# What the first tile's logits wait for, and the order of these logits, the rest columns and the third V tile in a fused attention/MLP kernel

## Chip, cores, metric

One core of one Trainium2 chip. The metric is device time of one execution in microseconds (us); lower is better. "TensorE" is PE in the profile, its weight loads are PEld, VectorE is DVE, ScalarE is ACT.

## The reference, cut to what matters

```python
q, k, v = split(x @ wqkv)                      # x: 2048 x 512, 32 heads of 16
pq = einsum("bhsd,hdf->bhsf", q, w_phi)        # logits of q
pk = einsum("bhsd,hdf->bhsf", k, w_phi)        # logits of k
phi = concat(softmax(p), softmax(-p))          # for both
kv, z = phi_k^T v, sum_s phi_k                 # linear attention
o  = (phi_q kv) / (phi_q z + 1e-6) @ wo
b  = relu(x @ w1) @ w2
return g * o + (1 - g) * b                     # g = sigmoid(x . gate_w)
```

`x @ wq @ w_phi` is computed as `x @ (wq w_phi)`: the kernel first folds `w_phi` into the q and k weights. (Each softmax has 15 free logits after subtracting the last one, so a folded matrix is 512 x 480.)

## The kernel before: the parts that matter

All engines' instructions are written in a fixed order; semaphores order them across engines. Blocks of 128 token rows are "tiles" (16 of them). The kernel's matmuls write into banks of a memory called PSUM (`PS`); an *evacuation* is the copy of such a result to a tile in the main on-chip memory (SBUF), from which the later matmuls read. A *folding* is one piece of the product `wq w_phi` or `wk w_phi`. Four pieces of TensorE work meet at the end of the start-up:

- `pre(i)`, eight foldings: `i` 0 to 3 give the q weights, 4 to 7 the k weights. Each has four matmuls of 120 columns into one PSUM bank (0, 1, 6, 7 in turn) and one evacuation to `WQK`, on DVE for even `i` and on ScalarE for odd `i`.
- `vtile(m)`: the V rows of tile `m`, four matmuls of 512 columns, one copy.
- `rest(0)`: the last 96 columns of the first MLP layer with the gate column for tokens 0 to 511, sixteen matmuls of 97 columns.
- `atile(0)`: the q and k logits of tile 0, eight matmuls of 480 columns, into PSUM bank 0 (q) and bank 1 (k).

```python
def pre(i):
    which, dt = i // 4, i % 4
    bank = (0, 1, 6, 7)[i % 4]
    dst = WQK[:, which, dt * DE:(dt + 1) * DE]
    ...                                   # four matmuls into PS[:, bank, 0:DE], event pm{i}
    if i % 2 == 0:
        p.op("dve", lambda e: e.tensor_copy(dst, PS[:, bank, 0:DE]), after=[f"pm{i}"], ev=f"pc{i}")
    else:
        p.op("act", lambda e: e.activation(dst, PS[:, bank, 0:DE], ACT.Copy),
             after=[f"pm{i}"], ev=f"pc{i}")
    free[bank] = [f"pc{i}"]               # who uses the bank next waits for this

def atile(m):
    first = xready(m // 4) + ([f"pc{i}" for i in range(8)] if m == 0 else [])
    order = [(dt, w) for dt in range(NDT) for w in range(2)]     # q, k, q, k, ...
    ...
    for i, (dt, which) in enumerate(order):
        p.op("pe", ...matmul(PS[:, which, 0:DE], XT[:, dt, tile], WQK[:, which, dt]),
             after=(first if i == 0 else []) + (free[which] if dt == 0 else []), ...)
    ...                                   # exponentials on ScalarE after all eight

# the order of the program there
hunit(0, 8); hunit(0, 9, "dve")
vtile(0, "dve"); vtile(1, "act", nextbank())
for i in range(4): pre(i)
rest(0)
for i in range(4, 8): pre(i)
vtile(2, "dve")
for m in range(NT): atile(m) ...
```

So the first logit matmul waits for all eight evacuations, because q and k alternate.

The softmax here doesn't subtract the row's maximum and nothing guards it: scores larger than these inputs give would overflow.

## Time and profile before

| | before |
|---|---|
| median of the first three runs | 147.69 us (147.18 to 147.95) |
| span of the profiled run | 146.8 us |
| PE busy | 143.2 us, 98% |
| share of PE in the chain that ended last | 95% |

From the page of the kernel before: the span, busy time by engine, and the chain that ended last by engine.

```profile
span 146.8 us, 2520 instructions
...
PE 143.2 (98%) x961; PEld 73.2 (50%) x978; DVE 92.3 (63%) x157; ACT 72.7 (49%) x125; POOL 52.0 (35%) x62
...
PE 95%; DMA 2%; DVE 1%; issue 1%; SPq 0%
```

TensorE is the limit from end to end. In such a kernel a change of order can win only what TensorE loses by waiting, so the question is where it waits. The view of waits of the kernel before has one line for the place of the change (who waited for whom: us in total, times, longest):

```profile
PEld PS L336 <- DVE WQK L321: 0.4, 1, 0.4
```

L336 is the logit matmuls, L321 the DVE evacuations of the folded weights. It is the weight *load* that waits 0.4 us, and loads normally run ahead of their matmuls, so most of it hides. The view names DVE, but see below: ScalarE's last evacuation ended later. The timeline of the kernel before shows the surroundings (start, duration, engine, line, operation, count, and in brackets the idle time before it):

```profile
16.23 1.00 PE L316 MATMUL PS<-Wbd,PHQ 128*128 128x120 bf16 x16
...
17.07 0.86 PE L294 MATMUL PS<-W,XT 128*128 128x97 bf16 x16
...
17.77 1.00 PE L316 MATMUL PS<-Wbd,PHQ 128*128 128x120 bf16 x16
...
18.18 1.22 DVE L321 CAST WQK<-PS 128x480 bf16<-128x480 f32 x2 [0.31 <-PE PS L316]
18.41 1.04 ACT L323 ACTIVATE WQK<-PS 128x480 bf16<-128x480 f32 x2
...
18.82 0.81 PE L411 MATMUL PS<-WV,XT 128*128 128x512 bf16 x3
19.56 1.34 PEld L336 LDWEIGHTS PS<-WQK,XT 128*128 128x128 bf16 x8 [0.42 <-DVE WQK L321]
19.59 1.78 PE L336 MATMUL PS<-WQK,XT 128*128 128x480 bf16 x8
```

Read down it: q folding, rest columns, k folding, V tile (one of its four records is missing), logits. The k evacuations end at 18.18 + 1.22 = 19.40 (DVE) and 18.41 + 1.04 = 19.45 (ScalarE), and the logits' load starts just behind, at 19.56. ScalarE came last: in the instruction records a semaphore instruction that waits for ScalarE stands in front of the load, and the load itself waits for DVE. The matmul line has no bracket, because a matmul's recorded duration (0.38 us for 512 columns) is longer than the time after which the next can start (0.216 us), so a short pause is covered by a modelled end. The chain of waits has the same blindness; of the kernel before it shows no pause there:

```profile
17.93 0.84 PE PS L316 x16
18.77 0.05 issue
18.82 0.81 PE PS L411 x3
19.63 1.74 PE PS L336 x8
```

The pause is seen only when the starts are compared: the last V matmul starts at 19.252, the first logit at 19.592, 0.340 us later, where 0.216 is the pitch, the usual time from one start to the next. That is 0.124 us lost.

### The profile page before, as it was taken

The numbers are of one execution on the slowest core, as the hardware profiler recorded it, in microseconds if no ns is written. First come the engines' busy times: TensorE is split into PE (matmuls) and PEld (weight loads), VectorE is DVE, ScalarE is ACT, GpSimd is POOL, SyncE is SP. The second block draws the span as 40 slices with busy tenths as digits, with TensorE's granted clock in tenths as the row PEclk, the third lists the DMA queues.
The fourth block names the chain that finished last, engine by engine and source line by source line (L and its number), as shares of the span: only waits on it lengthen the run. The fifth ranks groups of instructions, "written<-read, shape, count | busy, mean of one in ns | idle before, by whom it ended". The sixth has DMA issues, their size and how long they took to land.

```text
span 146.8 us, 2520 instructions
## 1 busy us (share of the span) xinstructions
PE 143.2 (98%) x961; PEld 73.2 (50%) x978; DVE 92.3 (63%) x157; ACT 72.7 (49%) x125; POOL 52.0 (35%) x62
## 2 busy tenths in 40 slices
PE   8999999999999999999999999999999999999994
PEld 3444744444545545555645555554444444444443
DVE  3327746777688778678698976675444555555342
ACT  3307547887778778877878863022222111111150
POOL 2040001788768678787868820300000000000000
DMA  6999991033449965335843531454343322322213
GB/s 197 295 258 214 180 263 23 0 71 71 76 86 304 178 198 92 71 71 107 43 107 71 107 71 21 90 107 110 74 94 82 75 71 67 80 71 74 71 44 106
DMA packets 45221, 16.12 MB, mean 110 GB/s; under 512 B 39352, under 2 KB 44568, under 8 KB 45208
## 3 DMA queue, kind: packets, MB, share of 16 engines
q1 hardware_dynamic: 45056, 15.92, 49.6%
q8 instruction: 8, 0.13, 0.4%
q10 hardware_dynamic: 152, 0.03, 0.1%
q14 instruction: 5, 0.04, 0.1%
HBM read 4.41 MB, written 2.10 MB: 44 GB/s over the span
## 4 chain that ended last, share of the span: by engine, by line
PE 95%; DMA 2%; DVE 1%; issue 1%; SPq 0%
PE PS L490 25%; PE PS L282 19%; PE PS L336 18%; PE PS L499 9%; PE PS L411 9%; PE PS L528 5%; PE PS L465 3%; PE PS L433 3%; DMA OT<-in_A_x_dram 2%; PE PS L294 2%; PE PS L316 1%; PE PS L239 1%; DVE WQK L513 1%; DVE XT L255 0%; SPq L162 0%
## 5 line engine op out<-in xcount | busy, mean ns | idle before, releaser
L490 PE MATMUL PS<-W,HT 128*128 128x512 bf16 (+4 forms) x181 | 40.0, 366 | 0.3
L379 POOL TENSOR_TENSOR EB<-EB,SC 128x1024 bf16<-128x1024 bf16 x15 | 28.9, 1927 | 25.0 <-DVE SC L377 25.0
L355 ACT ACTIVATE EB<-PS 128x480 bf16<-128x480 f32 (+1 forms) x44 | 30.1, 757 | 15.1 <-PE PS L336 15.1
L504 ACT ACTIVATE TFA<-PS,GT 128x512 bf16<-128x512 f32 x16 | 11.0, 687 | 42.7 <-PE PS L499 36.6
L282 PE MATMUL PS<-XT,W 128*128 128x512 bf16 x124 | 30.0, 379 | 0.2
L336 PE MATMUL PS<-WQK,XT 128*128 128x480 bf16 x128 | 28.5, 366 | 0.0
L375 DVE TENSOR_REDUCE ZB<-EB 128x64 f32<-128x1024 bf16 x15 | 18.3, 1220 | 14.0 <-ACT EB L355 14.0
L513 DVE SCALAR_TENSOR_TENSOR WQK<-PS,OMG,TFA 128x512 bf16<-128x512 f32 (+2 forms) x17 | 12.2, 719 | 23.6 <-ACT TFA L504 22.4
L490 PEld LDWEIGHTS PS<-W,HT 128*128 128x128 bf16 (+1 forms) x187 | 17.0, 98 | 17.4
L268 ACT ACTIVATE HT<-PS 128x512 bf16<-128x512 f32 x35 | 20.3, 616 | 7.6 <-PE PS L528 5.7
L336 PEld LDWEIGHTS PS<-WQK,XT 128*128 128x128 bf16 x128 | 12.5, 98 | 14.0 <-DVE WQK L321 0.4
L390 DVE TENSOR_REDUCE ZB<-EB 128x64 f32<-128x1024 bf16 x16 | 18.6, 1164 | 0.0
L282 PEld LDWEIGHTS PS<-XT,W 128*128 128x128 bf16 x128 | 12.0, 98 | 13.2
L399 POOL TENSOR_TENSOR EB<-EB,SC 128x512 bf16<-128x512 bf16 x16 | 16.9, 1056 | 1.3
L499 PE MATMUL PS<-WO,OT 128*128 128x512 bf16 x63 | 16.0, 378 | 0.1
L411 PE MATMUL PS<-WV,XT 128*128 128x512 bf16 x59 | 15.3, 378 | 0.3
L475 DVE TENSOR_TENSOR WQK<-PS,RDEN 128x512 bf16<-128x512 f32 x16 | 11.1, 691 | 0.5
L499 PEld LDWEIGHTS PS<-WO,OT 128*128 128x128 bf16 x64 | 6.1, 97 | 7.2
L421 ACT ACTIVATE VS<-PS 128x512 bf16<-128x512 f32 x14 | 8.5, 610 | 2.0 <-PE PS L411 2.0
L377 DVE RECIPROCAL SC<-ZB 128x64 f32<-128x64 f32 x16 | 8.9, 553 | 0.5
L528 PE MATMUL PS<-XT,W 128*128 128x512 bf16 x31 | 7.9, 400 | 0.1
L411 PEld LDWEIGHTS PS<-WV,XT 128*128 128x128 bf16 x64 | 5.5, 97 | 4.9
(57 smaller groups left out, 87.2 us busy)
## 6 DMA issues: line engine op xcount, KB each, us to landing
out_dram<-WQK SPq DMA_DIRECT2D x15, 128.0 KB, 1.7
W<-in_B_w_dram SPq DMA_DIRECT2D x3, 256.0 KB, 4.5
W<-in_B_w_dram SPq DMA_DIRECT2D x2, 384.0 KB, 5.3
OT<-in_A_x_dram SPq DMA_DIRECT2D x2, 256.0 KB, 3.0
WV<-in_A_wqkv_dram SPq DMA_DIRECT2D x1, 512.0 KB, 6.3
W<-in_B_w_dram SPq DMA_DIRECT2D x1, 512.0 KB, 4.5
WO<-in_A_wo_dram SPq DMA_DIRECT2D x2, 256.0 KB, 3.0
W<-in_B_w_dram SPq DMA_DIRECT2D x1, 352.0 KB, 5.8
```

The lines of the kernel that those rows point to most:

```text
L268: p.op("act", lambda e: e.activation(dst, src, ACT.Relu), after=[f"h{c}_{kt}"], ev=ev)
L282: p.op("pe", lambda e, t=t: e.matmul(PS[:, bank, :], W1[:, t, kt * P:(kt + 1) * P], XT[:, t, c * 512:(c + 1) * 512], start=(t == 0), stop= ...
L336: p.op("pe", lambda e, dt=dt, which=which: e.matmul(PS[:, which, 0:DE], XT[:, dt, m * P:(m + 1) * P], WQK[:, which, dt * DE:(dt + 1) * DE] ...
L355: p.op("act", lambda e: e.activation(dst, s_, ACT.Exp, scale=scale), after=[f"qk{m}"] + busy, ev=ev)
L375: p.op("dve", lambda e: e.tensor_reduce(zk, ek, AX.X, ALU.add), after=[emk, f"cst{b}"], ev=f"zk{m}")
L379: p.op("pool" if m < NT - 1 else "dve", lambda e: e.tensor_tensor(EB[:, b, 3, :].rearrange("p (g f) -> p g f", f=DH), EB[:, b, 2, :].rearr ...
L390: p.op("dve", lambda e: e.tensor_reduce(ZB[:, b, 0:64].rearrange("p (h s) -> p h s", s=2), bass.AP(tensor=EB, offset=base, ap=[[EBS, P], [ ...
L399: p.op("pool", lambda e: e.tensor_tensor(EB[:, b, 0, :].rearrange("p (h s f) -> p h s f", h=H, s=2)[:, :, 1, :], EB[:, b, 1, :].rearrange( ...
L411: p.op("pe", lambda e, dt=dt: e.matmul(PS[:, bank, :], XT[:, dt, m * P:(m + 1) * P], WV[:, dt, :], start=(dt == 0), stop=(dt == NDT - 1)), ...
L490: p.op("pe", lambda e, kt=kt, M=M: e.matmul(PS[:, bank, 0:n], HT[0:M, kt, m * P:(m + 1) * P], W2[0:M, kt, cs], start=(kt == 0), stop=(kt = ...
L499: p.op("pe", lambda e, t=t: e.matmul(PS[:, bank, :], OT[:, t, m * P:(m + 1) * P], WO[:, t, :], start=(t == 0), stop=(t == NDT - 1)), after ...
L528: p.op("pe", lambda e, u=u: e.matmul(PS[:, UB[u], :], W1[:, t, u * P:(u + 1) * P], XT[:, t, 0:512], start=(t == 0), stop=(t == NDT - 1)), ...
```

## The change

Its intent: let the first logits wait only for what they use. In tile 0 the four q matmuls come ahead of the four k matmuls, and each group waits for its own four evacuations. The q logits are written to bank 0, so through `free[0]` they also wait for that bank's last user, the first k folding `pre(4)`, to be evacuated. The third V tile moves between the two foldings, and the rest columns behind the k folding.

```diff
@@ atile
-            first = xready(m // 4) + ([f"pc{i}" for i in range(8)] if m == 0 else [])
+            first = xready(m // 4)
             order = [(dt, w) for dt in range(NDT) for w in range(2)]
             if m - 1 in split:
                 order = [(dt, w) for w in (1, 0) for dt in range(NDT)]
+            if m == 0:
+                order = [(dt, w) for w in (0, 1) for dt in range(NDT)]
             for i, (dt, which) in enumerate(order):
                 ...
-                    after=(first if i == 0 else []) + (free[which] if dt == 0 else []),
+                    after=(first if i == 0 else []) + (free[which] if dt == 0 else [])
+                    + ([f"pc{4 * which + c}" for c in range(4)] if m == 0 and dt == 0 else []),
@@ order of the program
         for i in range(4):
             pre(i)
-        rest(0)
+        vtile(2, "dve")
         for i in range(4, 8):
             pre(i)
-        vtile(2, "dve")
+        rest(0)
```

## The prediction

> **What bounds the kernel.** TensorE issue. The page gives PE busy 143.2 of 146.8 us (98%); the chain that ended last is 95% PE, and its pieces follow one another from 3.97 us on without a wait for another engine. In the instruction records a 512-column matmul starts 216 ns after the one before, a 480-column one 202 ns, a folding one (120 columns) 52 ns, a rest one (97 columns) 43 ns. (The Trainium skill, TensorE: Matmul & The Clock Gate, Back-to-back issue gap, gives N/2.4 + 2.5 ns when warm, 215.8 ns at 512; this trace agrees.)
>
> Comparing all start-to-start times with these pitches leaves one real gap after 12 us. (Others, 217 ns each with weight loads running on, are missing records.) It is where the change acts: the third V tile's last matmul starts at 19.25, so the first logit matmul is due at 19.47, but starts at 19.59: 0.12 us lost. It waits for the last two evacuations of folded k weights: DVE ends 19.40, ScalarE 19.45, then a semaphore instruction at 19.49, the load at 19.56, the matmul at 19.59. The view of waits has this as PEld waiting 0.4 us for DVE WQK L321, most of which is only a load that could not run ahead.
>
> **What the change does.** It removes and adds no work. From 16.23 (folding) the same matmuls run in another order: 16 x 52 + 4 x 216 + 16 x 52 + 16 x 43 ns = 3.24 us, so the first logit is due at 19.47 again. Worked out from the trace's durations:
> - V tile 17.07 to 17.93; its DVE copy starts 0.42 us after its last matmul starts (as before): 18.14 to 18.83.
> - k folding 17.93 to 18.77. DVE evacuates at 18.75-19.40 and 19.33-19.98 (behind the V copy, 0.6 us later than before); ScalarE at 18.58-19.15 and 19.03-19.62.
> - rest columns 18.77 to 19.47, taken by ScalarE from 19.66, where it was idle until 21.41.
> - q logits at 19.47: q weights are done by 17.95, but PSUM bank 0 was used by the first k folding, evacuated by DVE about 19.40. So the load still waits, just, for one semaphore: 19.47 to 19.52.
> - k logits due 0.81 us later, 20.28; their weights are done by 19.98.
>
> **On the critical path.** 0.07 to 0.12 us of TensorE time, nothing else. The first exponential moves from 21.41 to about 21.30. Everything behind is issue-bound with slack elsewhere: the next x chunk, read at 22.07, landed at 18.9, the k weights for the folding at 15.3. So the 0.1 us should survive to the end.
>
> **Predicted time.** 147.69 - 0.1 = 147.6 us, range 147.0 to 148.1 (three runs of before spread over 0.77 us, far more than the gain). Faster by over 2%: 1%; within 2%: 98%; slower by over 2%: 1%.
>
> **What would show it.** Right: in the timeline the first logit matmul near 19.5, the q ones followed without a pause by the k ones at 20.3; the wait of PEld for DVE WQK shrunk; span near 146.7. Wrong: a pause between q and k logits (k evacuation later than 20.2); a pause before the q logits as long as before; or the first exponential at 21.4.
>
> **What would make it wrong.** Bank 0 freed later than I work out, because the V copy delays the DVE queue: then the gain shrinks to nothing or a loss of 0.1 us. Input DMAs jittering more than here, where the old order had slack elsewhere. Later phases answering the 0.1 us shift with a new wait. None of these comes near 2%.

## The result, and the profile after

The change ran at 147.12 us median (146.99 to 147.26, six runs), before at 147.33 us (147.17 to 147.95, six runs). The ratio of the two is 0.9978, with a 95% interval of 0.9957 to 0.9999: "same" at 2%, barely below 1. Ratios here are the mean time of one kernel's fast runs over that of the other's of the same rounds, so not quite the ratio of the medians.

From the page of the changed kernel:

```profile
span 145.7 us, 2520 instructions
...
PE 142.1 (98%) x961; PEld 72.7 (50%) x978; DVE 92.2 (63%) x157; ACT 72.8 (50%) x125; POOL 52.0 (36%) x62
...
PE 97%; DVE 1%; issue 1%; ACT 0%; DVEq 0%
```

Its timeline at the same place (lines there are numbered 2 to 3 higher than before from the logits on: L338 is the logits, L414 the V tiles):

```profile
15.27 1.00 PE L316 MATMUL PS<-Wbd,PHQ 128*128 128x120 bf16 x16
...
16.11 1.03 PE L414 MATMUL PS<-WV,XT 128*128 128x512 bf16 x4
...
16.97 1.00 PE L316 MATMUL PS<-Wbd,PHQ 128*128 128x120 bf16 x16
17.17 0.69 DVE L422 CAST VS<-PS 128x512 bf16<-128x512 f32 x1 [0.27 <-PE PS L414]
17.59 1.03 ACT L323 ACTIVATE WQK<-PS 128x480 bf16<-128x480 f32 x2 [0.60 <-PE PS L316]
...
17.78 1.21 DVE L321 CAST WQK<-PS 128x480 bf16<-128x480 f32 x2
17.81 0.86 PE L294 MATMUL PS<-W,XT 128*128 128x97 bf16 x16
18.48 1.34 PEld L338 LDWEIGHTS PS<-WQK,XT 128*128 128x128 bf16 x8
18.51 1.78 PE L338 MATMUL PS<-WQK,XT 128*128 128x480 bf16 x8
```

The wait of PEld for L321 is gone from the view of waits; the load has no bracket. The last rest matmul starts at 18.462 and takes 0.043 us, so the first logit was due at 18.505; it started at 18.506. The DVE evacuation line, however, ends at 17.78 + 1.21 = 18.99, half a microsecond *after* the q logits began: it holds two evacuations, of which the q logits need only the first (bank 0, ended at 18.428). The chain of waits now runs rest columns into logits:

```profile
17.14 0.84 PE PS L316 x16
17.98 0.69 PE PS L294 x16
18.67 1.62 PE PS L338 x8
```

The whole span differs by 1.1 us, though. A table by stage, with starts of matmuls from the instruction records, says where:

| stage | before, us | change, us | difference |
|---|---|---|---|
| start of program to first folding matmul | 16.231 | 15.269 | -0.962 |
| first folding matmul to first q logit | 3.361 | 3.237 | -0.124 |
| first to last logit of tile 0 | 1.415 | 1.417 | +0.002 |
| last logit of tile 0 to end of last matmul | 123.803 | 123.802 | -0.001 |

The change acts in the second row. The first row is code that both kernels share word for word. Its beginning, in the timelines of TensorE of before and then of the change (L528 and L531 are the same line):

```profile
2.90 0.85 PE L239 MATMUL PS<-IDN,OT 128*128 128x128 bf16 x6
3.97 1.04 PE L239 MATMUL PS<-IDN,OT 128*128 128x128 bf16 x8 [0.22 <-DMA OT<-in_A_x_dram]
4.93 1.60 PE L528 MATMUL PS<-XT,W 128*128 128x512 bf16 x4
```

```profile
2.93 1.38 PE L239 MATMUL PS<-IDN,OT 128*128 128x128 bf16 x14
4.54 1.02 PE L531 MATMUL PS<-XT,W 128*128 128x512 bf16 x4 [0.23 <-ACT XT L258]
```

Before waited for the second half of the first x block, and its first four 512-column matmuls took 1.60 us instead of 1.02, because the array was still at its slow pitch (up to 0.427 us from start to start, against 0.216). They began 0.39 us later and took 0.58 us longer, which together accounts for the 0.96 us. The Trainium skill, TensorE: Matmul & The Clock Gate, "What's actually happening", says that the array runs at half clock until a free-running activity window of about 3.4 us has seen it busy, so that the changeover depends on where the window lies when the program starts. The trace agrees in kind: the last matmul at the slow pitch starts at 5.73 us in this profile of before and at 3.46 us in that of the change.

### The profile page after: what moved, and what is told of

It is laid out like the page before. It is cut to its first block, busy times and chain, and to the rows that moved or that the text cites. A ratio compares the mean times of both kernels' runs of the same rounds, so it can differ in the third digit from the quotient of the medians.

```text
span 145.7 us, 2520 instructions
## 1 busy us (share of the span) xinstructions
PE 142.1 (98%) x961; PEld 72.7 (50%) x978; DVE 92.2 (63%) x157; ACT 72.8 (50%) x125; POOL 52.0 (36%) x62
## 4 chain that ended last, share of the span: by engine, by line
PE 97%; DVE 1%; issue 1%; ACT 0%; DVEq 0%
PE PS L493 26%; PE PS L282 19%; PE PS L338 18%; PE PS L502 9%; PE PS L414 9%; PE PS L531 5%; PE PS L468 3%; PE PS L436 3%; PE PS L294 2%; PE PS L232 2%; PE PS L316 1%; PE PS L239 1%; DVE WQK L516 1%; DVE XT L255 0%; ACT XT L258 0%
## 5 line engine op out<-in xcount | busy, mean ns | idle before, releaser
L493 PE MATMUL PS<-W,HT 128*128 128x512 bf16 (+3 forms) x182 | 40.2, 366 | 0.3
L282 PE MATMUL PS<-XT,W 128*128 128x512 bf16 x124 | 30.2, 379 | 0.2
L338 PE MATMUL PS<-WQK,XT 128*128 128x480 bf16 x128 | 28.5, 366 | 0.0
L338 PEld LDWEIGHTS PS<-WQK,XT 128*128 128x128 bf16 x128 | 12.4, 98 | 13.6
L414 PE MATMUL PS<-WV,XT 128*128 128x512 bf16 x59 | 15.3, 379 | 0.3
L414 PEld LDWEIGHTS PS<-WV,XT 128*128 128x128 bf16 x64 | 5.5, 97 | 4.9
L468 PEld LDWEIGHTS PS<-KVNZ,PHQ 128*128 128x128 bf16 x128 | 6.1, 97 | 3.6
```

The lines of the kernel that those rows point to most:

```text
L282: p.op("pe", lambda e, t=t: e.matmul(PS[:, bank, :], W1[:, t, kt * P:(kt + 1) * P], XT[:, t, c * 512:(c + 1) * 512], start=(t == 0), stop= ...
L338: p.op("pe", lambda e, dt=dt, which=which: e.matmul(PS[:, which, 0:DE], XT[:, dt, m * P:(m + 1) * P], WQK[:, which, dt * DE:(dt + 1) * DE] ...
L414: p.op("pe", lambda e, dt=dt: e.matmul(PS[:, bank, :], XT[:, dt, m * P:(m + 1) * P], WV[:, dt, :], start=(dt == 0), stop=(dt == NDT - 1)), ...
L493: p.op("pe", lambda e, kt=kt, M=M: e.matmul(PS[:, bank, 0:n], HT[0:M, kt, m * P:(m + 1) * P], W2[0:M, kt, cs], start=(kt == 0), stop=(kt = ...
```

## The experiments

Call *stretch* the time from the start of the first folding matmul to the start of the last logit matmul of tile 0. It leaves the start-up out, and in all ten profiles what follows it lasted 123.80 us to within 0.003 us, so a difference in stretch is a difference in time.

The theory: TensorE lost 0.12 us waiting for k weights that the first matmul did not need; splitting the wait wins that and nothing else. Rivals: first, moving the V tile is what pays; second, grouping the logits by matrix, in any order, is what pays; third, the change does more than 0.12 us (the two spans differ by 1.1).

| kernel | first folding at | to first logit | stretch | span | median (runs) | ratio to before, 95% interval |
|---|---|---|---|---|---|---|
| before (first profile) | 16.231 | 3.361 | 4.776 | 146.80 | 147.33 (6) | 1 |
| the change (first profile) | 15.269 | 3.237 | 4.654 | 145.71 | 147.12 (6) | 0.9978 (0.9957 to 0.9999) |
| after_again | 15.355 | 3.236 | 4.654 | 145.80 | 147.44 (6) | 1.0001 (0.998 to 1.0023) |
| q_first_only | 15.995 | 3.237 | 4.655 | 146.44 | 147.36 (6) | 0.9997 (0.9969 to 1.0025) |
| swap_only | 15.247 | 3.781 | 5.209 | 146.25 | 147.87 (6) | 1.0035 (1.0006 to 1.0064) |
| k_first | 16.264 | 3.781 | 5.210 | 147.27 | 148.16 (6) | 1.0047 (1.0026 to 1.0069) |
| before_again | 15.846 | 3.360 | 4.774 | 146.42 | 147.33 (6) | 0.9995 (0.9969 to 1.0021) |
| before_all_dve | 15.765 | 5.077 | 6.505 | 148.06 | 149.27 (4) | 1.0109 (1.0073 to 1.0145) |
| qfirst_all_dve | 15.821 | 3.903 | 5.695 | 147.31 | 148.25 (4) | 1.0051 (1.0019 to 1.0083) |
| after_all_dve | 15.918 | 3.983 | 6.295 | 148.01 | 149.22 (4) | 1.0113 (1.0082 to 1.0143) |

The rows from after_again to k_first ran on one chip against before at 147.65 us median (11 runs), the last four on another against 147.33 us (11 runs). All results were correct.

### after_again: the change once more, no edit

> The changed kernel once more. Call 'stretch' the time from the start of the first folding matmul to the start of the last logit matmul of tile 0: 4.78 us in the first profile of before, 4.65 in that of the change. Theory (the gain is the one TensorE wait before the first logits, 0.12 us; the other 1.0 us between the two profiled spans is start-up variation ahead of 12 us, not the change): stretch 4.65 again, time 0.1 to 0.2 us under before. Rival (the change does something more, so that the 0.2 us median or the 1.1 us of span are its own): 0.4 us or more under before.

The stretch came out at 4.654 us again. The medians differ by 0.21 us, but the ratio is 1.0001 with an interval of 0.4%, so the times alone show no gain at all. The first ratio, 0.9978, must be read with that: its interval reaches to 0.9999, and 0.12 us of 147.5 is 0.0008.

### before_again: the kernel before once more, no edit

> The kernel before once more, unchanged: the null for the times and a second look at its start-up. Stretch (start of the first folding matmul to start of the last logit matmul of tile 0) 4.78 us again. Theory (the start-up ahead of the folding varies by chance from run to run, whatever the kernel): its first folding matmul starts somewhere between 15.2 and 16.3 us, as in the six profiles so far. Rival (the change shortened the start-up): 16.2 us again. Ratio of times 1.000, give or take 0.3%.

Against itself before gives 0.9995 with an interval of 0.5%: this is the grain of the timing. Its stretch was 4.774 us, its first folding at 15.846 us, within the expected range. Over all ten profiles that start lies between 15.247 us (swap_only) and 16.264 us (k_first), with the same code ahead of it in all ten; the two profiles of before alone differ by 0.385 us. So the 0.96 us of the first table lies within the scatter of the start-up, and no run shows more of a gain than 0.12 us: the third rival has nothing left to stand on.

### q_first_only: the logit part alone

```diff
@@ against the change
-        vtile(2, "dve")
+        rest(0)
         for i in range(4, 8):
             pre(i)
-        rest(0)
+        vtile(2, "dve")
```

> Only the q-first part: q logits wait for q weights only, the rest columns stay between the two foldings and the third V tile stays last. Theory (splitting the wait is what pays, the reordering of V tile and rest columns is not needed): no wait is left before the first logits, stretch 4.65 us, time as the change within 0.1 us. Rival (the V tile put ahead is needed to free the wait): stretch 4.7 to 4.8 as before.

The stretch was 4.655 us, as the whole change within 0.001 us. From its timeline:

```profile
17.94 1.22 DVE L321 CAST WQK<-PS 128x480 bf16<-128x480 f32 x2 [0.31 <-PE PS L316]
...
19.02 1.53 PEld L338 LDWEIGHTS PS<-WQK,XT 128*128 128x128 bf16 x8
19.23 1.78 PE L338 MATMUL PS<-WQK,XT 128*128 128x480 bf16 x8
```

Here the load even runs its usual 0.21 us ahead of the matmul, where in the whole change it comes 0.03 us ahead. The moved V tile is not needed for the gain. This is the experiment that decides against the first rival.

### swap_only: the reordering alone

```diff
@@ against before
-        rest(0)
+        vtile(2, "dve")
         for i in range(4, 8):
             pre(i)
-        vtile(2, "dve")
+        rest(0)
```

> Only the other part: third V tile between the foldings, rest columns behind, all eight evacuations still waited for before the first logit. Theory: DVE's last k evacuation now ends 0.5 us after the logits are due, so TensorE waits about 0.6 us there: stretch 5.2 to 5.3 us, time 0.5 us over before. Rival (V tile ahead is what pays): stretch under 4.78, time under before.

The stretch was 5.209 us, 0.433 us longer than before, and the time rose by 0.35%. In its timeline the logits wait openly, even by the modelled ends:

```profile
17.15 0.69 DVE L419 CAST VS<-PS 128x512 bf16<-128x512 f32 x1 [0.27 <-PE PS L411]
...
17.76 1.21 DVE L321 CAST WQK<-PS 128x480 bf16<-128x480 f32 x2
...
19.02 1.33 PEld L336 LDWEIGHTS PS<-WQK,XT 128*128 128x128 bf16 x8 [0.53 <-DVE WQK L321]
19.03 1.79 PE L336 MATMUL PS<-WQK,XT 128*128 128x480 bf16 x8 [0.38 <-DVE WQK L321]
```

The V copy (0.69 us) stands in DVE's queue in front of the k evacuations, which end at 18.97, while the logits were due at 15.247 + 3.236 = 18.48. So this half of the change, alone, is a loss.

### k_first: the change with the two groups exchanged

```diff
@@ against the change
-                order = [(dt, w) for w in (0, 1) for dt in range(NDT)]
+                order = [(dt, w) for w in (1, 0) for dt in range(NDT)]
```

> The change with k logits ahead of q logits in tile 0, everything else kept, so the wait is still split but in the other order. Theory: the k weights are evacuated last, so TensorE waits about 0.55 us before the first logit: stretch about 5.2 us, time about 0.5 us over the change. Rival (grouping the logits by weight matrix, or the split of the wait as such, pays whichever comes first): stretch 4.65.

5.210 us, as swap_only. The split wait and the grouping are the same as in the change; only the matrix that comes first differs. From its timeline:

```profile
18.77 1.21 DVE L321 CAST WQK<-PS 128x480 bf16<-128x480 f32 x2
...
20.04 1.33 PEld L338 LDWEIGHTS PS<-WQK,XT 128*128 128x128 bf16 x8 [0.53 <-DVE WQK L321]
20.05 1.79 PE L338 MATMUL PS<-WQK,XT 128*128 128x480 bf16 x8 [0.38 <-DVE WQK L321]
```

Grouping as such wins nothing, which decides against the second rival.

### before_all_dve, qfirst_all_dve, after_all_dve: the wait made long

In each, DVE does all eight evacuations, so that they end much later.

```diff
@@ pre(i), against before, q_first_only and the change
-            if i % 2 == 0:
+            if True:
                 p.op("dve", lambda e: e.tensor_copy(dst, PS[:, bank, 0:DE]), ...)
```

> The kernel before with all eight evacuations of folded weights on DVE, so that the wait before the logits is made much longer. Worked out from 0.57 us between DVE evacuations: the last ends 5.1 us after the first folding matmul starts, the logits were due at 3.9, so the wait is 1.2 us and the stretch about 6.6 us; time about 1.8 us over before.

> The same all-DVE evacuation with the q-first part alone. Theory (the split hides as much of the evacuation's lateness as four q logits last, 0.81 us): q logits start when due, 3.9 us after the first folding matmul, then a pause of about 0.4 us before the k logits, stretch about 5.8 us: 0.8 us under the all-DVE before, seven times the 0.12 us of the real change. Rival (the split saves a fixed 0.1 us or so, say one semaphore instruction): stretch 6.4 to 6.5 us.

> The same all-DVE evacuation with the whole change. Theory (the V tile ahead puts its 0.6 us DVE copy in front of the k evacuations, harmless only while DVE has slack): the q logits wait 0.2 to 0.3 us for bank 0, the k logits for the last evacuation, stretch about 6.4 us, 0.6 us over the q-first part alone. Rival (V tile ahead and rest columns behind help, or do nothing): stretch 5.8 us or less.

Stretches were 6.505, 5.695 and 6.295 us, each about 0.1 us under what was expected; DVE evacuations followed one another every 0.565 us where 0.57 had been assumed, and without the V copy ahead the last ended 5.02 us after the first folding matmul where 5.1 had been expected. The folding matmuls themselves wait for banks here, so the first q logit of the second kernel starts 3.903 us after the first folding matmul and not 3.237. The logits in the three timelines, before with all evacuations on DVE first:

```profile
20.84 1.33 PEld L336 LDWEIGHTS PS<-WQK,XT 128*128 128x128 bf16 x8 [1.50 <-DVE WQK L321]
20.84 1.79 PE L336 MATMUL PS<-WQK,XT 128*128 128x480 bf16 x8 [1.01 <-DVE WQK L321]
```

then with the q logits ahead:

```profile
19.72 0.97 PE L338 MATMUL PS<-WQK,XT 128*128 128x480 bf16 x4
...
20.90 0.98 PE L338 MATMUL PS<-WQK,XT 128*128 128x480 bf16 x4 [0.20 <-DVE WQK L321]
```

and with the whole change:

```profile
18.60 0.68 DVE L422 CAST VS<-PS 128x512 bf16<-128x512 f32 x1
...
19.20 2.34 DVE L321 CAST WQK<-PS 128x480 bf16<-128x480 f32 x4
...
19.90 0.98 PE L338 MATMUL PS<-WQK,XT 128*128 128x480 bf16 x4
...
21.59 0.98 PE L338 MATMUL PS<-WQK,XT 128*128 128x480 bf16 x4 [0.71 <-DVE WQK L321]
```

Splitting the wait won 6.505 - 5.695 = 0.810 us, which is the four q matmuls (4 x 0.202 us) that now run while the k weights are still being evacuated. That is the most the split can win, and in the real kernel only 0.12 us of waiting was there to be won. With DVE loaded like this the moved V tile and rest columns cost 6.295 - 5.695 = 0.600 us, about the time of its copy.

## Why the prediction was right

Point by point, times of the change shifted by the 0.962 us by which its start-up was shorter:

- *"One real gap after 12 us", 0.12 us.* Right: 0.124 us lost before, 0.001 us after, and every later stage equal to 0.002 us. The gain reached the end: what follows the logits took 123.80 us in all ten profiles. (A side remark of the prediction is not right: the chain of before is not free of other engines from 3.97 us on, it has 0.42 us of DVE at 6.67 us. That lies ahead of the change and alters nothing.)
- *q logits at "19.47 to 19.52", load waiting "just".* 18.506 + 0.962 = 19.468, and its load followed the end of bank 0's evacuation (18.428) by 0.052 us. That this evacuation binds, and not a q weight, shows plainly in after_all_dve: there the last q evacuation ended 2.763 us after the first folding matmul, the first k one (bank 0) at 3.926, and the first q logit started at 3.983.
- *The evacuations.* Predicted for DVE 18.75 to 19.40 and 19.33 to 19.98; measured 18.74 to 19.39 and 19.31 to 19.96. For ScalarE predicted 18.58 to 19.15 and 19.03 to 19.62; measured 18.55 to 19.12 and 19.02 to 19.59. The method was to take each duration from the trace and push it through the new queue order.
- *k logits without a pause, first exponential about 0.1 us earlier.* Right: the eight logits are 0.202 us apart, and the first exponential starts 0.123 us earlier, 20.325 + 0.962 = 21.287 against 21.410.
- *Within 2%; 147.6 us, 147.0 to 148.1.* 147.12 is inside, near the lower end. That proves little: 0.1 us is less than the scatter of the runs, and the range would have held without any gain. The stretch is what bears the prediction out. The 0.1 us was the right gain; the level it was subtracted from was not exact, since 147.69 was the median of three runs and six gave 147.33. *"Span near 146.7"* missed (145.7) for a like reason: it took one profile's start-up for the rule.
- *A point the prediction did not make:* it costed the whole change and never its halves. One half carries the gain; the other is neutral at best.

The old wait also shows what the 0.124 us were made of. The Trainium skill, Perfetto Trace Analysis, "Identifying Dependency Chains", notes that an instruction waiting for several engines may have a semaphore instruction in front. Before has one: ScalarE's evacuation ended at 19.447, the semaphore instruction ran at 19.485 (0.051 us), the load at 19.561, the matmul at 19.592, 0.145 us after the evacuation (0.145 us in before_again too). The k weights were thus ready 0.021 us *before* the first logit was due (19.468); what came late was the hand-over. Where TensorE waited openly for DVE with no semaphore instruction in the last step (swap_only, k_first and the three all-DVE kernels), it was 0.057 to 0.058 us from the end of the evacuation to the matmul. An estimate from these numbers: had before's last step been as short, the loss would have been 19.447 + 0.057 - 19.468 = 0.036 us. So about 0.09 of the 0.124 us would be due to the semaphore instruction coming last, and only the rest to the k weights. qfirst_all_dve rules out that the split saves only such a fixed amount, but no run says how the 0.124 us divide (one could keep the common wait and let DVE's evacuation end last); the change removes both.

None of the versions beats the change by a measured amount. q_first_only equals it in stretch with a smaller edit and with 0.6 us more room on DVE.

## What to carry to other kernels

When a stage begins with several weights that are prepared just ahead of it, let each matmul wait only for what it reads, and put first those whose data is ready first; the gain is the wait that is there, and at most the work that can be put in front. A wait can cost time even for data that are ready in time: here the hand-over alone took 0.057 to 0.145 us. Before moving other work into the gap, ask in whose queue its evacuation lands: here a V tile put ahead on TensorE put a copy ahead of the critical evacuations on DVE. For effects of a tenth of a per cent compare starts in a stage that leaves the start-up out; total times and modelled ends hide them.

## What the Trainium skill lacked or had wrong

- TensorE: Matmul & The Clock Gate, "Back-to-back issue gap": its formula N/2.4 + 2.5 ns held for streams of weight load and matmul pairs (216 ns at 512 columns, 202 at 480, 52 at 120, 43 at 97, each with its own load), though the page calls it the gap of an isolated matmul. The figures it gives for such streams, about 131 ns at 512 and 81 ns at 128, were not seen as a steady pitch in any run here (216 at 512; 56 at 128, once the slow pitch was over).
- The same page, Part 1: it puts the changeover to the fast clock at about 4 us of sustained activity, give or take 0.5, run by run. In these ten profiles the first matmul started at 0.38 us and the last slow one between 3.46 and 5.98 us. The activity had pauses (0.43 us at 3.5 us in before), so this doesn't show the page wrong; but in a real start-up the changeover scattered more. The first folding matmul moved over 1.02 us in these profiles (15.247 to 16.264), 0.7% of the span and eight times the effect studied.
- Perfetto Trace Analysis, "Tensor Engine Instruction (MATMUL, LD_WEIGHTS)": it says that matmul ends are estimated. It does not say what follows for a pause: here 0.124 us showed neither as idle time of the matmul nor in the chain of waits, only in the starts.
- No page that I found gives the time from an evacuation to the matmul that waits for it: 0.057 to 0.058 us from DVE's end where TensorE waited openly and no semaphore instruction came last, 0.145 us from ScalarE's end with a semaphore instruction in between.
